# Unread opening products, early first operands and column-tiled filling products in a transformer-block forward and backward kernel

## The chip, the core and the metric

The kernel runs on one core of one Trainium2 chip. The metric is the device time of one execution in microseconds (us), as the median over several runs; lower is better.

Engine names in the profile: PE is the matrix engine (PEld its weight loads), DVE the vector engine, ACT the scalar engine, POOL is GpSimd, and SP the engine whose queue issues most transfers (SPq; in every view of it below they go out in the program's order). "Step", "round", "slot" and "row" are explained with the code.

## The reference

One transformer block with attention and a gated MLP in parallel, its output and all six gradients, in bf16: S = 2048 tokens, D = 448, 16 heads of 28, F = 1792.

```python
def _fwd_reference(A_x, A_wqkv, A_wo, B_x, B_w_gate, B_w_up, B_w_down):
    x = A_x
    xn = _layernorm(x, axis=-1)
    return x + _A_ref(xn, A_wqkv, A_wo) + _B_ref(xn, B_w_gate, B_w_up, B_w_down)
# _A_ref: qkv = xn @ wqkv; softmax(q k^T / sqrt(28)) v; @ wo
# _B_ref: (silu(xn @ w_gate) * (xn @ w_up)) @ w_down

def reference(A_x, A_wqkv, A_wo, B_w_gate, B_w_up, B_w_down, B_x, grad_out):
    _out, _vjp = jax.vjp(_f, A_x, A_wqkv, A_wo, B_w_gate, B_w_up, B_w_down)
    return (_out, *_vjp(grad_out))
```

## The kernel before

The kernel has three stages. An *opening* (to about 46 us) normalises x and projects the first Q, K and V. The *forward* (to about 606 us) runs 256 slots of scores, exponential and P times V, while "units" of other matrix work (MLP products, weight gradients) fill the gaps of PE. The *backward* runs 512 steps. A *row* of step k is the recomputed scores of step k and the products dO V^T of step k-1; ACT takes the exponential, DVE makes `ds`, PE makes dV and dK from both (`kv`). Four steps make a *round*, in which three of the four `ds` tiles are transposed by DMA and one on PE; the transposed tiles feed dQ (`dq`). The rest of PE's time goes to filling units again (`genb` tiles). Between forward and backward lies the *turn*.

The turn: six big loads (2.9 MB), then the first four rows, placed between the last five forward units; the row needs these loads.

```python
    def turn_loads():
        ...
        SP.dma_start(out=new_k(0, 0)[:], in_=KD_d[0, 0])
        for qc in range(4):
            SP.dma_start(out=new_q(0, qc)[:], in_=QD_d[0, qc])
        SP.dma_start(out=new_k(0, 1)[:], in_=KD_d[0, 1])
    ...
    for u in last[:-5]:
        run(u())
    k = n = 0
    for u in last[-5:]:
        for _ in u():
            n += 1
            if n in (8, 17, 25, 32):
                row(k); ew(k); k += 1
    K0 = k
    sp_flush()                     # two stores of the last transposed forward tile (odT)
    fwd.close()
    ...
    for x in pend:                 # DMA transposes of the first ds tiles, held back until here
        x()
    fT = bk.tile([P, 4, 2, 4, P], BF16, name="dsp", bufs=1)
    drip(("f",), [(fT[:, a:a + 2], fT_d[:, a:a + 2]) for a in (0, 2)], 10)
```

A transposed forward tile is stored by the same queue that later transposes `ds`, and the stores wait there for their own transpose to land (0.8 us in the profile of this kernel, 3.8 in that of the changed one), with everything issued after them behind:

```python
    def dst_dma(b, ds, qi):        # three of four ds tiles of a round
        SP.dma_start_transpose(out=dsT[b][:, qi]..., in_=ds[:]...)
    def ew(k):
        ...
        ds = dss[k - 1] = kq.tile([P, 2, 512], BF16, name="ds_sb", bufs=10)
        for j in range(2):
            DVE.tensor_tensor(out=ds[:, j], in0=dps.pop((k - 1, j))[:], in1=est[k - 1][:, j], op=ALU.mult)
        if qi < 2 or qi == 2 and b < NB // 4 - 1:
            pend.append(...) if bk is None else dst_dma(b, ds, qi)
```

A filling unit, one of five kinds (here the first kind in the backward, whose operand is `fT`):

```python
    def late_dw(c):
        have(("f",))
        ps = ps_g.tile([P, 2, P], FP32, name="genb")
        for t in range(NT):
            PE.matmul(ps[:dn], lhsT=xn_sp[:, t, d0:d0 + dn], rhs=fT[:, t // 4, :, t % 4, :], ...)
```

The softmax here doesn't subtract the row's maximum and nothing guards it: scores larger than these inputs give would overflow.

## Time and profile before

| | value |
|---|---|
| median of 3 runs | 1441.15 us (1439.99 to 1442.68) |
| span in the profile, granted clock | 1440.1 us, 0.985 |
| PE, ACT, DVE busy | 92%, 88%, 80% |
| exponential of the last forward slot / first ds / ds of step 511 | 606.52 / 617.22 / 1393.6 us |

Busy shares are averages over stages with different limits; the prediction below shows the stage lines and the turn of this profile. One more view of it matters, which I had not read closely before predicting: SP's own queue at the turn, in order of issue (start, how long the issues took, queue, line, operation, output<-input, count).

```profile
619.96 1.29 SPq L200 DMA_TRANSPOSE odT<-od  x1
...
622.78 0.32 SPq L206 DMA_DIRECT2D OT_d<-odT  x1
...
623.67 4.26 SPq L829 DMA_TRANSPOSE dsT<-ds_sb  x3
627.99 1.08 SPq L769 DMA_DIRECT2D dsp<-fT_d  x2
629.17 5.95 SPq L829 DMA_TRANSPOSE dsT<-ds_sb  x3
```

The reader is to see that the transpose of odT goes out at 619.96, when its operand is there, and the stores behind it wait 0.8 us more for odT to land.

### The profile page before, as it was taken

The page shows a single profiled execution, that of the slowest core. Times are in us where ns is not written, and L with a number is a line of the kernel's source. Part 1 is how long each engine was busy: PE and PEld are TensorE (multiplying, and loading weights), DVE is VectorE, ACT ScalarE, POOL GpSimd, SP SyncE. Part 2 cuts the span into 40 slices and gives each one's busy share as a digit, 9 for nine tenths or more (in the row PEclk, how much of TensorE's full clock was granted, in tenths as well). Part 3 has the DMA queues.
Part 4 walks back from the last instruction along what each step waited for, and adds up shares of the span by engine and source line. Part 5 has one row for each costly group of instructions (what it writes and reads, how often), then busy time and mean ns, then how long its engine had stood idle before and what let it go on. Part 6 is the DMA issues. An engine that isn't in the chain of part 4 may idle for free. (4 is left out here: it accounts for less than half of the span.)

```text
span 1440.1 us, 34682 instructions
## 1 busy us (share of the span) xinstructions
PE 1326.3 (92%) x12647; PEld 541.0 (38%) x12708; DVE 1151.8 (80%) x1997; ACT 1261.5 (88%) x2193; POOL 403.6 (28%) x561
## 2 busy tenths in 40 slices
PE   5889999999999999889999999999999999999996
PEld 2333333333333333333333434433443444444343
DVE  6667757666676676578998998888889999989988
ACT  5789988988889999869989989899989999989974
POOL 6464524464334454111112112201111011010006
PEclk9999999999999999989999999999999999999998
DMA  5796956796678586799999999999999999999971
GB/s 154 181 199 165 235 122 160 187 195 164 146 162 192 147 172 145 178 234 226 226 213 217 232 220 188 196 209 229 228 173 194 209 223 230 201 191 203 198 142 60
DMA packets 681179, 271.69 MB, mean 189 GB/s; under 512 B 606424, under 2 KB 655824, under 8 KB 681008
## 3 DMA queue, kind: packets, MB, share of 16 engines
q1 hardware_dynamic: 672576, 255.35, 87.1%
q0 software_dynamic: 7024, 13.82, 4.1%
q8 instruction: 100, 1.64, 0.5%
q14 instruction: 71, 0.58, 0.1%
q10 hardware_dynamic: 1408, 0.30, 0.1%
HBM read 65.09 MB, written 60.36 MB: 87 GB/s over the span
## 5 line engine op out<-in xcount | busy, mean ns | idle before, releaser
L842 DVE TENSOR_TENSOR ds_sb<-db,e_sb 128x512 bf16<-128x512 f32 x1024 | 646.8, 684 | 51.3 <-issue 21.1
L836 ACT ACTIVATE e_sb<-sb 128x512 bf16<-128x512 f32 x1024 | 554.8, 611 | 60.4 <-PE db L820 44.5
L612 ACT ACTIVATE eT<-s_w 128x1024 bf16<-128x1024 f32 x256 | 263.5, 1029 | 46.1 <-PE s_ps L609 43.1
L614 ACT ACTIVATE eT<-s_ps 128x512 bf16<-128x512 f32 x512 | 280.4, 612 | 0.0
L820 PE MATMUL db<-kd,qd 32*128 32x512 bf16 x1024 | 234.4, 384 | 8.2 <-DVE ds_sb L842 7.4
L812 PE MATMUL sb<-kd,qd 32*128 32x512 bf16 x1024 | 210.4, 387 | 5.1 <-DMA qd<-QD_d 3.3
L961 POOL TENSOR_TENSOR dq_acc<-dq_acc,dq_st 128x256 f32<-128x256 f32 x64 | 46.2, 721 | 455.4 <-ACT dq_st L959 455.4
L919 PE MATMUL acc<-ds_sb,qd 128*32 128x512 bf16 x1024 | 161.0, 391 | 0.0
L915 PE MATMUL acc<-e_sb,qd 128*32 128x512 bf16 x1024 | 158.8, 391 | 1.3 <-DVE dw_o L528 1.3
L902 ACT COPY dsT<-db 128x1024 bf16<-128x1024 bf16 x128 | 130.1, 1016 | 14.6 <-PE db L897 13.9
L380 POOL TENSOR_TENSOR nn<-nn,ag 128x512 f32<-128x512 f32 x56 | 71.2, 1271 | 252.2 <-DVE ag L378 243.7
L609 PE MATMUL s_ps<-QQ,KK 32*128 32x512 bf16 x512 | 125.4, 385 | 3.9
L1128 PE MATMUL genb<-wguT,dau_c 128*128 128x448 bf16 x448 | 117.5, 355 | 6.3 <-ACT dq_st L959 3.9
L609 PE MATMUL s_w<-QQ,KK 32*128 32x512 bf16 x512 | 100.3, 387 | 13.1 <-ACT eT L612 10.4
L812 PEld LDWEIGHTS <-qd 32*128 32x128 bf16 x1024 | 48.2, 91 | 149.4 <-issue 140.3
L421 PE MATMUL gen<-xn_t,f_sp 128*128 128x448 bf16 x416 | 91.8, 354 | 2.6 <-DVE nn L395 1.7
L421 PEld LDWEIGHTS <-f_sp 128*128 128x128 bf16 x640 | 55.7, 98 | 75.0 <-issue 31.9
L946 PE MATMUL genb<-dsT,kd 128*32 128x256 bf16 x2048 | 79.5, 275 | 1.9 <-DVE dqT L955 0.6
L897 PE MATMUL db<-ident_bf,ds_sb 128*128 128x128 bf16 x1032 | 79.4, 220 | 1.1 <-DVE ds_sb L842 1.1
L897 PEld LDWEIGHTS <-ds_sb 128*128 128x128 bf16 x1032 | 68.3, 99 | 24.1 <-issue 5.3
L451 PE MATMUL gen<-eT,VS 128*32 128x512 bf16 x1024 | 68.4, 384 | 5.5 <-DVE nn L395 3.3
L381 POOL TENSOR_TENSOR nn<-nn,tt 128x512 f32<-128x512 f32 x56 | 72.0, 1286 | 4.4
(167 smaller groups left out, 1911.0 us busy)
## 6 DMA issues: line engine op xcount, KB each, us to landing
F_d<-hda SPq DMA_DIRECT2D x56, 384.0 KB, 3.1
dau_c<-F_d SPq DMA_DIRECT2D x24, 512.0 KB, 4.4
qd<-QD_d SPq DMA_DIRECT2D x16, 512.0 KB
kd<-KD_d SPq DMA_DIRECT2D x16, 384.0 KB, 4.0
dsT<-ds_sb SPq DMA_TRANSPOSE x383, 4.3
dc<-dqkvT_d SPq DMA_DIRECT2D x12, 384.0 KB, 3.9
h_c<-F_d SPq DMA_DIRECT2D x8, 512.0 KB, 4.4
wT_d<-wT_f SPq DMA_DIRECT2D x14, 256.0 KB, 3.6
```

The source lines that it names most:

```text
L421: PE.matmul(ps[:, :D], lhsT=fsp[fc][:, t // 4, w, t % 4, :], rhs=rhs[:, t, :], start=(t == 0), stop=(t == NT - 1))
L609: PE.matmul(sp4[hh], lhsT=KK[g][r:r + HP, kt * P:(kt + 1) * P], rhs=QQ[g][r:r + HP, qsl], start=True, stop=True, tile_position=(r, 0))
L612: ACTE.activation(out=e2[0][:], in_=wide[:], func=ACT.Exp, scale=SCALE)
L614: ACTE.activation(out=e2[1][:, j], in_=sp4[2 + j], func=ACT.Exp, scale=SCALE)
L812: PE.matmul(s_ps[:], lhsT=qside[g, qc][r:r + HP, 0, qi * P:(qi + 1) * P], rhs=kside[g, kc][r:r + HP, 0, :], start=True, stop=True, tile_po ...
L820: PE.matmul(d_ps[:], lhsT=qside[g, qc][r:r + HP, 1, qi * P:(qi + 1) * P], rhs=kside[g, kc][r:r + HP, 1, :], start=True, stop=True, tile_po ...
L836: ACTE.activation(out=est[k][:, j], in_=sps.pop((k, j))[:], func=ACT.Exp, scale=SCALE)
L842: DVE.tensor_tensor(out=ds[:, j], in0=dps.pop((k - 1, j))[:], in1=est[k - 1][:, j], op=ALU.mult)
L897: PE.transpose(ps[:, c, :], ds[:, c // 4, (c % 4) * P:(c % 4 + 1) * P], ident_bf[:])
L902: ACTE.copy(out=o, in_=ps[:])
L915: PE.matmul(a[r:r + HP, :], lhsT=sp4[:, 1, r:r + HP], rhs=e[:, j, :], start=first, stop=last, tile_position=(0, r), skip_group_check=True)
L919: PE.matmul(a[r:r + HP, :], lhsT=sp4[:, 0, r:r + HP], rhs=ds[:, j, :], start=first, stop=last, tile_position=(0, r), skip_group_check=True)
```

## The change

Three parts. *Opening*: 24 products that nobody reads at the start, and 3 more before each of three projections, with the aim of a full clock of PE early on (granted 0.83 from 15 to 46 us in the profile before). *Turn*: 512 KB of operands for the first four rows are loaded at forward slot 240 into a tile of their own; row 0 goes ahead of the last six forward units; some DVE work of these units goes to ACT and POOL. *Tiles*: from step 160 on, a filling product that follows dV/dK is issued as four products on 32 columns each, so that the tile shape of PE needn't change between them (dV/dK to fill took 0.32 us, dV/dK to dV/dK of one shape 0.22).

```diff
+    def warm(ps, n):
+        for _ in range(n):
+            PE.matmul(ps[:], lhsT=ident_bf[:], rhs=ident_bf[:]...to_broadcast([P, 4, P]), start=True, stop=True)
...
+    warm(genx.tile([P, 512], FP32, name="gen"), 24)
...
-        proj(1, c + 1)
+        proj(1, c + 1, pre=3)
...
+        if i == NS - 16:
+            sp_flush()
+            first4 = wk.tile([P, S], BF16, name="qk_sp", bufs=1)[:]...
+            SP.dma_start(out=first4[:, 0:2], in_=KD_d[0, 0, :, 0:2])
+            SP.dma_start(out=first4[:, 2:4], in_=QD_d[0, 0, :, 0:2])
...
+            ks, qs = (first4[:, 0], first4[:, 2]) if k < 4 else (kside[g, kc][:, 0], qside[g, qc][:, 0])
...
-    for u in last[:-5]:
+    for u in last[:-6]:
         run(u())
-    k = n = 0
-    for u in last[-5:]:
+    n = 0
+    K0 = 5
+    row(0)
+    ew(0)
+    k = 1
+    for u in last[-6:]:
         for _ in u():
             n += 1
-            if n in (8, 17, 25, 32):
+            if n in (4, 20, 24, 32):
...
+    def mm(ps, lhsT, rhs, start, stop):
+        if not split:
+            PE.matmul(ps, lhsT=lhsT, rhs=rhs, start=start, stop=stop, skip_group_check=True)
+            return
+        for c in range(0, lhsT.shape[1], HP):
+            PE.matmul(ps[c:c + HP], lhsT=lhsT[:, c:c + HP], rhs=rhs, start=start, stop=stop,
+                      tile_position=(0, c), skip_group_check=True)
...
+        split = m > 1 and k >= 160
```

(The five unit kinds call `mm`; the last od unit's copy and product go to ACT and POOL, its small operations to POOL, the last dW_o copy to ACT.)

More of the change, by code (lines that the diff above doesn't have):

```diff
@@ L267, in qkv_open, with qkv_unit @@
         VS[g] = wk.tile([P, NT, P], BF16, name="VS")
-    def qkv_unit(g, tq, sc, act=False):
+    def warm(ps, n):
+        for _ in range(n):
+            PE.matmul(ps[:], lhsT=ident_bf[:], rhs=ident_bf[:].unsqueeze(1).to_broadcast([P, 4, P]), start=True, stop=True)
+    def qkv_unit(g, tq, sc, act=False, pre=0):
         if g not in QQ:
@@ L274, in qkv_unit @@
         ps = new_gen([P, 512], FP32, name="gen")
+        warm(ps, pre)
         for c in range(4):
@@ L503, in mid3 @@
         dl = wk.tile([P, 3, 16], FP32, name="dl")
-        DVE.tensor_copy(out=dOl, in_=prod[:])
-        DVE.tensor_tensor(out=prod[:], in0=prod[:], in1=t[:, 0].rearrange("p q (h r) -> p (q h) r", r=HP), op=ALU.mult)
+        end = (g, qc) == (G - 1, 3)
+        (ACTE.copy if end else DVE.tensor_copy)(out=dOl, in_=prod[:])
+        (POOL if end else DVE).tensor_tensor(out=prod[:], in0=prod[:], in1=t[:, 0].rearrange("p q (h r) -> p (q h) r", r=HP), op=ALU.mult)
         yield 0
@@ L508, in mid3 @@
         yield 0
-        DVE.tensor_scalar(out=dl[:, 1, :], in0=dl[:, 0, :], scalar1=-1.0, scalar2=None, op0=ALU.mult)
-        DVE.tensor_copy(out=dOl[:, :, 28], in_=dl[:, 1, :])
-        DVE.tensor_tensor(out=dl[:, 2, :], in0=dl[:, 1, :], in1=dOl[:, :, 28], op=ALU.subtract)
-        DVE.tensor_copy(out=dOl[:, :, 29], in_=dl[:, 2, :])
+        eng = POOL if (g, qc) == (G - 1, 3) else DVE
+        eng.tensor_scalar(out=dl[:, 1, :], in0=dl[:, 0, :], scalar1=-1.0, scalar2=None, op0=ALU.mult)
+        eng.tensor_copy(out=dOl[:, :, 28], in_=dl[:, 1, :])
+        eng.tensor_tensor(out=dl[:, 2, :], in0=dl[:, 1, :], in1=dOl[:, :, 28], op=ALU.subtract)
+        eng.tensor_copy(out=dOl[:, :, 29], in_=dl[:, 2, :])
         tT = wk.tile([P, 2, 4, P], BF16, name="odT")
@@ L527, in dwo_unit @@
         o = wk.tile([P, D], BF16, name="dw_o", bufs=1)
-        DVE.tensor_copy(out=o[:], in_=ps[:, :D])
+        (ACTE.copy if g == G - 1 else DVE.tensor_copy)(out=o[:], in_=ps[:, :D])
         for hh in range(4):
@@ L632, in T, with proj @@
             run(T_unit(xnT, xn_t, t))
-    def proj(tq, sc, act=False):
-        run(qkv_unit(0, tq, sc, act))
+    def proj(tq, sc, act=False, pre=0):
+        run(qkv_unit(0, tq, sc, act, pre))
     def stats4(cc):
@@ L728 @@
         slot(i)
+        if i == NS - 16:
+            sp_flush()
+            first4 = wk.tile([P, S], BF16, name="qk_sp", bufs=1)[:].rearrange("p (a s) -> p a s", a=4)
+            SP.dma_start(out=first4[:, 0:2], in_=KD_d[0, 0, :, 0:2])
+            SP.dma_start(out=first4[:, 2:4], in_=QD_d[0, 0, :, 0:2])
         if kq is None and i > NS - 8 and not fill.stream and fill.cur is None:
@@ L811, in row @@
                 r = HP * (2 * hp + j)
-                PE.matmul(s_ps[:], lhsT=qside[g, qc][r:r + HP, 0, qi * P:(qi + 1) * P],
-                          rhs=kside[g, kc][r:r + HP, 0, :], start=True, stop=True, tile_position=(r, 0))
+                PE.matmul(s_ps[:], lhsT=qs[r:r + HP, qi * P:(qi + 1) * P],
+                          rhs=ks[r:r + HP], start=True, stop=True, tile_position=(r, 0))
                 sps[k, j] = s_ps
@@ L816, in row @@
             g, hp, kc, qc, qi = steps[k - 1]
+            ks, qs = (first4[:, 1], first4[:, 3]) if k <= 4 else (kside[g, kc][:, 1], qside[g, qc][:, 1])
             for j in range(2):
@@ L819, in row @@
                 r = HP * pv(2 * hp + j)
-                PE.matmul(d_ps[:], lhsT=qside[g, qc][r:r + HP, 1, qi * P:(qi + 1) * P],
-                          rhs=kside[g, kc][r:r + HP, 1, :], start=True, stop=True, tile_position=(r, 0))
+                PE.matmul(d_ps[:], lhsT=qs[r:r + HP, qi * P:(qi + 1) * P],
+                          rhs=ks[r:r + HP], start=True, stop=True, tile_position=(r, 0))
                 dps[k - 1, j] = d_ps
@@ L864 @@
                 k += 1
-    K0 = k
     sp_flush()
@@ L880, in late_dw @@
         for t in range(NT):
-            PE.matmul(ps[:dn], lhsT=xn_sp[:, t, d0:d0 + dn], rhs=fT[:, t // 4, :, t % 4, :],
-                      start=(t == 0), stop=(t == NT - 1))
+            mm(ps[:dn], xn_sp[:, t, d0:d0 + dn], fT[:, t // 4, :, t % 4, :], t == 0, t == NT - 1)
             if t < NT - 1:
@@ L890 @@
     dq_acc = bk.tile([P, S // 2], FP32, name="dq_acc", bufs=1)
+    split = False
+    def mm(ps, lhsT, rhs, start, stop):
[5 more added lines that the diff above has]
+                      tile_position=(0, c), skip_group_check=True)
     def tr_unit(b):
@@ L1010, in dwq_unit @@
         for t in range(NT):
-            PE.matmul(ps[:dn, :], lhsT=xn_sp[:, t, d0:d0 + dn], rhs=dsp[g][:, t].rearrange("p k r -> p (k r)"),
-                      start=(t == 0), stop=(t == NT - 1))
+            mm(ps[:dn, :], xn_sp[:, t, d0:d0 + dn], dsp[g][:, t].rearrange("p k r -> p (k r)"), t == 0, t == NT - 1)
             if t < NT - 1:
@@ L1066, in y_unit @@
         tsl = slice(ti * P, (ti + 1) * P)
-        mm = [(ych[ch, half][:, i, tsl], wd_sb[:, half * NH + i, :]) for i in range(NH)]
+        ops = [(ych[ch, half][:, i, tsl], wd_sb[:, half * NH + i, :]) for i in range(NH)]
         if half:
-            mm += [(ych[ch, 3][:, i, tsl], wo_sb[:, i, :]) for i in range(G)]
+            ops += [(ych[ch, 3][:, i, tsl], wo_sb[:, i, :]) for i in range(G)]
         ps = ps_g.tile([P, 512], FP32, name="genb")
-        for i, (l, r) in enumerate(mm):
-            PE.matmul(ps[:, :D], lhsT=l, rhs=r, start=(i == 0), stop=(i == len(mm) - 1))
-            if i < len(mm) - 1:
+        for i, (l, r) in enumerate(ops):
+            mm(ps[:, :D], l, r, i == 0, i == len(ops) - 1)
+            if i < len(ops) - 1:
                 yield 189
@@ L1127, in dx_unit @@
         for i in range(n):
-            PE.matmul(ps[:, :D], lhsT=d[:, i // 2, i % 2, tsl], rhs=dxs["w", fq][:, i // 2, i % 2, :],
-                      start=(i == 0), stop=(i == n - 1))
+            mm(ps[:, :D], d[:, i // 2, i % 2, tsl], dxs["w", fq][:, i // 2, i % 2, :], i == 0, i == n - 1)
             if i < n - 1:
@@ L1171, in dc_unit @@
         for i in range(3 * G - 3):
-            PE.matmul(ps[:, :D], lhsT=dcs[t // 4][:, i, (t % 4) * P:(t % 4 + 1) * P], rhs=dxs["wq"][:, i, :],
-                      start=(i == 0), stop=(i == 3 * G - 4))
+            mm(ps[:, :D], dcs[t // 4][:, i, (t % 4) * P:(t % 4 + 1) * P], dxs["wq"][:, i, :], i == 0, i == 3 * G - 4)
             if i < 3 * G - 4:
@@ L1270 @@
             fill_step(R3)
+    split = False
     while stream:
```

## The prediction

> **What bounds the kernel now.** I read the page first, then the busy time by stage, then the timeline at the opening, at the turn from forward to backward, and in single rounds of the backward. The page says that no engine is alone at its limit, and where the slow clock lies.
>
> ```profile
> PE 1326.3 (92%) x12647; PEld 541.0 (38%) x12708; DVE 1151.8 (80%) x1997; ACT 1261.5 (88%) x2193; POOL 403.6 (28%) x561
> PEclk9999999999999999989999999999999999999998
> ```
>
> The reader is to see that the clock is nearly full everywhere: whatever warm-up gives is confined to a few short dips. By stage (columns: busy time and instructions of PE, weight loads, DVE, ACT, POOL; granted clock, DMA share, GB/s):
>
> ```profile
> 15.00:46.00 31.00, 24.28 (x161) 8.48 (x163) 19.47 (x44) 23.29 (x36) 15.34 (x13) 0.83 0.28 58
> 46.00:606.00 560.00, 520.86 (x3766) 201.41 (x3822) 374.34 (x644) 504.45 (x785) 248.19 (x332) 1.00 0.76 175
> 606.00:640.00 34.00, 26.37 (x220) 9.58 (x220) 23.24 (x42) 20.12 (x37) 3.23 (x6) 0.85 0.84 211
> 880.00:1395.00 515.00, 494.76 (x5680) 208.44 (x5678) 470.60 (x798) 472.25 (x881) 65.18 (x97) 0.99 1.08 202
> ```
>
> The forward (46 to 606) has PE and ACT at 93% and 90%. The turn (606 to 640) is the hole: ACT idles 13.9 of 34 us, DVE 10.8. In the backward PE is at 96%, DVE and ACT at 91 to 92%: three engines in lockstep, so time taken from one of them mostly becomes waiting there. The turn's timeline shows the wait that the change aims at (start, length, engine, line, operation, output<-input; brackets: idle before it, releaser):
>
> ```profile
> 610.02 1.91 SPq L724 DMA_DIRECT2D qd<-QD_d  x4
> ...
> 614.10 0.39 PE L812 MATMUL sb<-kd,qd 32*128 32x512 bf16 x2 [3.27 <-DMA qd<-QD_d]
> ...
> 614.52 1.09 ACT L836 ACTIVATE e_sb<-sb 128x512 bf16<-128x512 f32 x2 [6.00 <-PE sb L812]
> ...
> 617.22 1.28 DVE L842 TENSOR_TENSOR ds_sb<-db,e_sb 128x512 bf16<-128x512 f32 x2
> ...
> 622.98 0.39 PE L915 MATMUL acc<-e_sb,qd 128*32 128x512 bf16 x2 [1.28 <-DVE dw_o L528]
> ```
>
> The first backward scores wait for a load issued 4 us earlier, and the first dV/dK product waits for a DVE copy queued behind other DVE work. One backward round (four steps, 5.63 us):
>
> ```profile
> 1147.94 2.48 DVE L842 TENSOR_TENSOR ds_sb<-db,e_sb 128x512 bf16<-128x512 f32 x4 [0.16 <-issue]
> 1147.95 0.38 PE L915 MATMUL acc<-e_sb,qd 128*32 128x512 bf16 x2
> ...
> 1148.27 0.36 PE L1128 MATMUL genb<-wguT,dau_c 128*128 128x448 bf16 x1
> 1148.57 0.39 PE L812 MATMUL sb<-kd,qd 32*128 32x512 bf16 x2
> 1148.57 0.49 PE L820 MATMUL db<-kd,qd 32*128 32x512 bf16 x2
> 1148.99 0.93 PE L1128 MATMUL genb<-wguT,dau_c 128*128 128x448 bf16 x4
> ```
>
> From a dV/dK pack to the filling product is 0.32 us; from one dV/dK pack to the next (128x32 tiles both) 0.22; also from dV/dK to dQ, which has 128x32 tiles too, 0.22. So changing the tile shape costs about 0.10 us. The 0.49 and the 0.42 us up to the next fills show that the following row lost 0.10 us on its second db tile.
>
> [...] the dQ packs here (four 32-column tiles, 256 wide) follow each other at 0.109 us[...], so loads of narrow tiles stay hidden. [...] granted 0.50 in stretches of 3.4 or 6.8 us (20.6 to 27.4, 41.1 to 44.5, 614.5 to 617.9, 624.8 to 628.2, 631.6 to 635.0).
>
> **The change, part by part.**
>
> *Opening products.* 24 unread 512-column products run from about 1.4 us, and 3 more before each of three projections. The first transposes start at 9.35 us. At half speed a product of 512 columns takes 0.427 us (the first eight projection products took 2.83 us in all, at spacings of 0.42), at full speed 0.216. [...] The 8 projection products then save 8 x 0.21 = 1.7 us, but DVE has statistics before the Q copy, so the first scores (15.46) come about 1.1 us sooner. That is then lost: the transposes at 18.58 and 20.42 wait for GpSimd's normalisation, whose chain begins with a queue of weight loads and does not depend on PE. What can last is the clock from 20.6 to 27.4 and 41.1 to 44.5, where PE is busy 5.9 and 2.9 us and ACT waits for it (2.5 and 2.4 us before the exponentials at 24.15 and 43.85). Removing both dips would give 3 us at most; but the dip at 20.6 follows a sparse stretch that lies before the first three extra products, and if the clock is down they cost 3 x 0.21 = 0.6 us more. I book 1.5 us.
>
> *Early first operands.* Two loads of 256 KB at the last 16th forward slot serve the first four rows; row 0 moves ahead of the transposes at 609.73. It can go at about 609.0 (the last forward products end at 608.9) instead of 614.10: 5.1 us. DVE's first ds then follows the od product: start 611.4 instead of 617.2. Also taken from DVE in this chain: 0.43 + 0.69 (copy and product), 0.17 + 0.20 + 0.18 + 0.20 (small ones), 0.61 (dw_o) = 2.5 us, to ACT and POOL. In DVE's new order, od, 2 ds, prod 0.69, 2 ds, reduce 0.61, 2 ds, with ds at 0.62: the sixth ds ends at 611.4 + 3.7 + 1.3 = 616.4, against 622.4 before: 6.0 us. Row 4 still needs the big loads (its query tile is the second, the first was there at 614.1; I estimate 615), but they are no longer first. The 16 dW_o products end about 617.4, ACT copies, and the first dV/dK starts near 618.2 instead of 622.98: 4.8 us. One row more is done by then (five, not four), and the dips at 624.8 and 631.6, which follow idle PE, may go or shrink (up to 1.7 us each). I book 6.5 us.
>
> *Column tiles.* Built, the PE order shows 424 filling products (240, 80 and 20 of 448 columns, 84 of 384) cut in tiles, 1,230 extra products and as many extra loads. They belong to some 80 units, each with one dV/dK-to-fill change removed: 80 x 0.10 = 8 us of PE time. A pack may take up to 0.01 us longer than one wide product (dV/dK packs come at 0.216 or 0.226), and the exit to the next row 0.01. What reaches the end depends on the kind of round, which I sorted by length. Rounds of 5.63 us (19): DVE idles only 0.16, at a point upstream of the fill, and the next row waits 0.10 for DVE: gain 0. Rounds of 5.91 (11, ACT copies the unit): the same 0.10 us wait swallows it: 0, or -0.02. Rounds of 5.69 (9): 0.07 is swallowed, some 0.05 gained as they approach 5.63: 0.5. Ends of a K chunk (13, 6.3 to 6.7 us): the change of shape lies in the last step of the round and ACT then waits 0.52 for the next row: 0.07 each, 0.9. Weight-gradient rounds (12, 6.4 us, PE waits 0.1): 0.05 each, 0.6. Rounds with transposes: 0. Sum 1.5 to 2, booked as 1.5.
>
> Sum: 1.5 + 6.5 + 1.5 = 9.5 us; 1441.2 - 9.5 = 1431.7.
>
> **The rivals.** (a) *Column tiles pay in full.* PE waits for others only about 34 of 760 us in the backward (640 to 1400, the view of waits), which speaks for PE as the bound; then 8 instead of 1.5 us: 1425. Against it stands DVE's idle of 0.16 us in the commonest round. (b) *Column tiles cost.* [...] The dQ packs speak against it. (c) *The turn's gain is taken back.* Row 4 and the dW_o products sit behind the db buffers, which DVE frees, and behind the 2.9 MB of big loads; if the first dV/dK only comes at 620, 3 us remain: 1435. For it: the DMA is at 382 GB/s just then. (d) *The opening is hidden wholly* behind GpSimd and DMA, or the extra products run at half clock: 1433.
>
> **Range and chances.** The turn is the surest part (4 to 8.5), the opening -0.5 to 3.5, the tiles -1 to 6. Together a central 9 to 10 and 8 times in 10 between 4 and 15: 1426 to 1437. Two per cent is 28.8 us; all three parts at their upper ends give 18. So faster by over 2%: 0.02; within: 0.97; slower: 0.01.
>
> **What would show it.** In the changed profile: the first backward scores near 609 without a DMA wait, the first ds near 611.5, the first dV/dK near 618 (each shifted by what the opening gave); dV/dK to fill 0.22 us, and the next row's wait grown from 0.10 to about 0.20 in the 5.63 us rounds, which keep their length; 6.4 us rounds shortened by 0.05; clock below 0.95 between 20 and 27 gone or not, decides the opening. I am wrong if the rounds of 5.63 us shorten by 0.1, if tile packs follow at much over 0.19 us, or if the first dV/dK comes no earlier than 621.

The 1.7 us of the eight projection products supposed that the 24 bring the clock up before them; when that would be was not shown. (In the changed profile the 24 start 0.43 us apart up to 4.25 us and 0.216 after it, the first record of a granted clock, 1.00, is at 4.19 us, and from 11.0 to 14.4 us it is 0.50.) Two statements stand on measured numbers. That loads of narrow tiles stay hidden: the 0.109 us between dQ packs of 256 columns is half of the 0.216 of a 512-column product. That dips follow idle PE: in the 3.4 us before the five dips PE was busy 73%, 59%, 13%, 49% and 76%.

## The result, and the profile after

The changed kernel took 1442.3 us (median of 4 runs, 1441.2 to 1442.9); the kernel before took 1440.6 beside it (4 runs, 1439.4 to 1442.7). The ratio is 1.001, 95% interval 0.9992 to 1.0027: the same. I had predicted 1431.7 with a range of 1426 to 1437, so the 9.5 us that I had summed up are not there.

The page of the changed kernel, busy time and granted clock in 40 slices:

```profile
PE 1339.5 (93%) x13971; PEld 556.0 (39%) x13971; DVE 1148.8 (80%) x1990; ACT 1260.8 (88%) x2195; POOL 406.6 (28%) x566
PEclk9999999999999999989999999999999999999998
```

The clock row reads as before. By stage (columns as in the prediction):

```profile
15.00:46.00 31.00, 25.78 (x205) 10.03 (x205) 21.55 (x48) 25.18 (x39) 15.56 (x13) 1.00 0.31 66
46.00:606.00 560.00, 526.16 (x3800) 200.65 (x3801) 371.96 (x642) 502.87 (x782) 248.90 (x332) 1.00 0.75 175
606.00:640.00 34.00, 24.82 (x202) 9.88 (x198) 19.09 (x32) 19.49 (x35) 4.74 (x10) 0.85 0.88 211
880.00:1395.00 515.00, 494.00 (x6870) 218.44 (x6859) 469.88 (x796) 470.50 (x881) 65.30 (x97) 0.99 1.11 202
```

In the opening the granted clock is 1.00 from 15 to 46 us in this trace, 0.83 in the kernel before (ten later traces with these products do not repeat that, see below). But the turn, where the change aimed at the holes, is emptier than before: PE 24.82 us instead of 26.37, DVE 19.09 instead of 23.24 (some 2.5 us of DVE's work went to ACT and POOL by the change itself), at the same mean clock of 0.85. Its timeline says where:

```profile
608.48 0.39 PE L826 MATMUL sb<-qk_sp 32*128 32x512 bf16 x2
...
610.92 1.28 DVE L857 TENSOR_TENSOR ds_sb<-db,e_sb 128x512 bf16<-128x512 f32 x2
...
617.99 0.39 PE L826 MATMUL sb<-kd,qd 32*128 32x512 bf16 x2 [2.55 <-DMA qd<-QD_d]
...
621.50 0.61 PE L942 MATMUL acc<-e_sb,qd 128*32 128x512 bf16 x2 [0.62 <-ACT dw_o L535]
...
632.48 0.58 PE L913 MATMUL genb<-dsp,xn_t 128*128 128x256 bf16 x2 [2.98 <-DMA dsp<-fT_d]
```

The first scores come at 608.48 without a wait and the first `ds` at 610.92, as predicted. Then row 4 waits for the big loads until 617.99, the first dV/dK starts at 621.50, only 1.5 us earlier than before, and a wait that the kernel before did not have stands at 632.48: the first filling product waits 2.98 us for its own operand `fT`. SP's queue in the changed kernel, to lay beside the one above:

```profile
616.66 1.38 SPq L200 DMA_TRANSPOSE odT<-od  x1
...
622.50 0.32 SPq L206 DMA_DIRECT2D OT_d<-odT  x1
...
623.41 4.11 SPq L844 DMA_TRANSPOSE dsT<-ds_sb  x3
627.58 1.06 SPq L782 DMA_DIRECT2D dsp<-fT_d  x2
628.74 7.57 SPq L844 DMA_TRANSPOSE dsT<-ds_sb  x3
```

The transpose of odT is issued 3.3 us earlier, but it lands no earlier (its stores go at 622.50 instead of 622.78). The big loads are in flight then; that they hold it up was not tested. So the first transpose of `ds` is issued at 623.41 instead of 623.67, and `fT` is loaded at 627.58 instead of 627.99. PE, ACT and DVE are 6 us ahead, and the queue isn't: the backlog between a first `ds` and its transpose grew from 6.45 to 12.49 us.

In the common backward round after step 160 the tiles do what was worked out:

```profile
1144.60 0.38 PE L942 MATMUL acc<-e_sb,qd 128*32 128x512 bf16 x2
...
1144.82 0.36 PE L916 MATMUL genb<-wguT,dau_c 128*32 128x448 bf16 x4
...
1145.16 0.55 PE L835 MATMUL db<-kd,qd 32*128 32x512 bf16 x2
...
1145.64 0.94 PE L916 MATMUL genb<-wguT,dau_c 128*32 128x448 bf16 x16
```

dV/dK to the fill is 0.22 us instead of 0.32, sixteen 32-column products of 448 take 0.94 us as four whole ones did (0.93), so no cost of their loads shows, and the next row's second tile takes 0.55 instead of 0.49: the time won becomes waiting for DVE, and the round is 5.64 us long.

### The profile page after: what moved, and what is told of

Its sections match the earlier page's. It is cut to its first block, busy times and chain, and to the rows that moved or that the text cites. A ratio compares the mean times of both kernels' runs of the same rounds, so it can differ in the third digit from the quotient of the medians. Undisturbed runs are those within 1.5% of the kernel's fastest.

```text
span 1440.4 us, 37274 instructions
## 1 busy us (share of the span) xinstructions
PE 1339.5 (93%) x13971; PEld 556.0 (39%) x13971; DVE 1148.8 (80%) x1990; ACT 1260.8 (88%) x2195; POOL 406.6 (28%) x566
## 5 line engine op out<-in xcount | busy, mean ns | idle before, releaser
L616 PE MATMUL s_w<-QQ,KK 32*128 32x512 bf16 x512 | 99.7, 385 | 12.3 <-ACT eT L619 10.4
L616 PEld LDWEIGHTS <-KK 32*128 32x128 bf16 x1024 | 29.2, 91 | 114.4 <-issue 111.7
```

The lines of the kernel that those rows point to most:

```text
L616: PE.matmul(sp4[hh], lhsT=KK[g][r:r + HP, kt * P:(kt + 1) * P], rhs=QQ[g][r:r + HP, qsl], start=True, stop=True, tile_position=(r, 0))
```

## The experiments

**How to read them.** Single runs of one kernel scattered far more here than in the first result: the kernel before, run 44 times on three chips, took 1437.5 to 1448.0 us, and each kernel's own six runs spread by 2 to 5 us (standard deviation). A median alone can't settle 2 us. So I cut every profiled run at the same marks: the exponential of forward slot 32 and of slot 255 (the last), and the `ds` of backward steps 0, 12, 36, 152 and 511. The columns from "ds 0" to "ds 152" count from the exponential of slot 255; "queue" is the issue of the first transpose of `ds`; "half" is the time between slot 255 and step 152 in which the records give a granted clock of 0.50.

| kernel | slot 32 | slot 255 | ds 0 | queue | ds 12 | ds 36 | ds 152 | half | 152 to 511 | ratio (95%) |
|---|---|---|---|---|---|---|---|---|---|---|
| before | 99.7 | 606.5 | 10.7 | 17.2 | 31.2 | 65.5 | 244.4 | 13.7 | 542.7 | 1 |
| changed | 94.6 | 606.1 | 4.8 | 17.3 | 33.3 | 67.4 | 244.1 | 17.1 | 542.1 | 1.001 (0.9992-1.0027) |
| e1 turn only | 99.9 | 607.9 | 4.8 | 15.7 | 30.7 | 67.0 | 245.6 | 23.9 | 540.9 | 1.0017 (0.9994-1.0040) |
| e2 opening only | 98.9 | 607.9 | 11.5 | 18.0 | 32.7 | 68.5 | 243.3 | 27.3 | 543.4 | 1.0036 (1.0017-1.0054) |
| e3 tiles only | 100.1 | 611.6 | 11.1 | 17.5 | 32.0 | 67.4 | 244.2 | 17.1 | 540.2 | 1.0008 (0.9985-1.0031) |
| e4 fill from 13 | 100.2 | 611.2 | 4.8 | 16.9 | 24.8 | 66.4 | 245.9 | 20.5 | 540.0 | 1.0020 (1.0001-1.0040) |
| e5 fT first | 96.8 | 611.0 | 4.8 | 18.7 | 27.6 | 70.4 | 248.8 | 30.7 | 538.7 | 1.0029 (1.0007-1.0051) |
| e6 fT first, row 4 late | 98.2 | 607.8 | 4.8 | 18.0 | 27.7 | 68.5 | 248.6 | 23.9 | 541.3 | 1.0017 (0.9991-1.0044) |
| e7 = e6, no opening | 100.9 | 608.2 | 4.8 | 17.1 | 26.7 | 68.0 | 243.7 | 23.9 | 538.5 | 0.9969 (0.9946-0.9992) |
| e8 24 products only | 99.3 | 609.4 | 12.1 | 18.5 | 33.3 | 67.4 | 245.4 | 13.7 | 540.9 | 1.0000 (0.9976-1.0023) |
| e9 changed, PE transposes | 98.5 | 608.1 | 4.8 | 17.2 | 29.0 | 63.9 | 244.8 | 23.9 | 540.3 | 0.9984 (0.9955-1.0012) |
| e10 before, PE transposes | 98.9 | 609.0 | 11.1 | 17.5 | 32.5 | 68.5 | 244.5 | 20.5 | 547.7 | 1.0013 (0.9990-1.0037) |
| e11 changed, stores moved | 99.8 | 609.4 | 4.8 | 13.7 | 29.0 | 63.3 | 242.8 | 17.1 | 538.5 | 1.0009 (0.9985-1.0034) |
| e12 all relief, no opening | 100.5 | 611.0 | 4.8 | 13.5 | 25.1 | 63.2 | 241.2 | 10.2 | 543.9 | 0.9970 (0.9945-0.9996) |
| e13 before, fewer loads | 98.6 | 607.7 | 10.9 | 17.4 | 31.8 | 66.1 | 239.1 | 17.1 | 543.4 | 0.9978 (0.9956-1.0000) |
| e14 changed, fewer loads | 97.4 | 607.8 | 4.8 | 16.8 | 31.1 | 68.3 | 243.5 | 34.1 | 540.6 | 0.9972 (0.9951-0.9993) |
| e15 changed again | 97.5 | 608.1 | 4.8 | 16.8 | 32.5 | 67.0 | 243.6 | 30.7 | 542.7 | 1.0011 (0.9979-1.0043) |
| e16 candidate | 96.2 | 603.0 | 4.8 | 13.5 | 24.0 | 65.7 | 242.0 | 20.5 | 546.1 | 0.9960 (0.9940-0.9981) |
| e17 changed, no opening | 101.1 | 609.7 | 4.8 | 15.9 | 30.6 | 67.2 | 244.3 | 23.9 | 539.7 | 0.9987 (0.9960-1.0014) |
| e18 e16 + opening | 97.6 | 612.9 | 4.8 | 13.5 | 25.9 | 66.6 | 247.1 | 23.9 | 539.0 | 0.9997 (0.9967-1.0027) |

**Part of the scatter is half-clock stretches.** Over the 152 runs of the experiments, each group's mean taken out, time and mean granted clock correlate at -0.59, so about a third of the variance goes with the clock. The stretches are 3.41 us long or a multiple of it (but for the last, which the span's end cuts), on a grid whose phase differs from run to run (edges at 13.79, 20.62 and 27.44 us in the profile before, at 4.19, 11.02 and 14.43 in the changed one). I laid that grid through all 20 traces and took PE's busy share in each full-speed window: after a window of 0.9 or more the clock was halved 0 times out of 6191, after 0.8 to 0.9 27 times out of 975, after 0.6 to 0.7 58 of 186, after less than 0.5 49 of 58. One such window cost 1.4 to 1.5 us where it falls on the tail (in the changed profile PE is busy all through it): the tail behind step 511 takes 46.5 to 46.7 us in the kernels without a window there and 47.9 to 48.1 in those with one. So a stall of 2 to 3 us costs itself, and may cost up to 1.5 us more right after it (an estimate from these counts and the tail).

### The three parts alone, and a later first fill (one set)

**e1_turn_only.** The changed kernel without its opening products and with the products whole:

```diff
-    warm(genx.tile([P, 512], FP32, name="gen"), 24)
...
-        proj(1, c + 1, pre=3)
+        proj(1, c + 1)
...
-        split = m > 1 and k >= 160
+        split = False
```

> Only the turn part is applied (early first operands, rows moved ahead, DVE work moved to ACT and POOL); no opening products, no column tiles. Theory T1 (the turn's gain is handed back at the first filling product, which now waits about 3 us for its own operand, the load of fT): the first ds comes about 6 us earlier than in the kernel before, round 8 about 3 us earlier, and by step 16 nothing of it is left; total within 1.5 us of the kernel before, ratio 0.999 to 1.001. Rival R1 (the prediction's: the turn pays its 6.5 us and another part costs them): 1434, ratio 0.9955. Rival R2 (what is left of it is lost to half-clock stretches that fall by chance): between -3 and +1, and step 16 about 3 us early.

Measured: 1443.4 us (before 1440.0 in this set), ratio 1.0017. The first `ds` is 5.9 us nearer to the last forward exponential, by step 12 the lead is 0.6 us, by step 36 it is gone. The first fill waited 3.37 us for `fT`. T1 holds; R1 (1434) is out. R2 is out as the main cause, since the lead is lost at that wait, though it has half-clock windows behind it.

**e2_open_only.** The kernel before plus `warm`, the 24 products and `pre=3`, as in the diff above.

> Only the 24 opening products and the three times 3 before projections are added to the kernel before. Theory T2 (the forward is held by something that does not depend on its start, so it swallows the early lead): about 5 us ahead at forward slot 64, less than 1 us ahead at the last forward slot; total within 1 us, ratio 0.9993 to 1.0007. Prediction's step: 1.5 us gained, ratio 0.999. Rival R3 (the products cost): +1 us or more, with a half-clock stretch in the Q and K projections that delays slot 0.

Measured: 1445.0 us, ratio 1.0036: slower than any of the expectations but R3's. The profiled run shows a lead of 0.8 us at slot 32, 0.9 at slot 64 (T2 wanted 5 there) and none by slot 255. More on this below.

**e3_tiles_only.** The kernel before plus `mm` and `split`, as in the diff above.

> Only the column tiles from step 160 on are applied. Theory T3: they pay 2 to 3.5 us as the round-by-round working said (0.05 to 0.11 in the longer rounds, none in the common one): total 1438 to 1439.5, ratio 0.9975 to 0.9985. Rival (b) of the prediction, tiles cost: +1 us or more. Rival (a), they pay in full: -8 us, ratio 0.9945.

Measured: 1441.1 us (1437.4 to 1445.7), ratio 1.0008 with an interval of 0.9985 to 1.0031: inconclusive in total time. By the marks the stretch in which tiles exist, step 152 to 511, is 2.4 us shorter than in the kernel before (540.2 instead of 542.7). Over all 20 traces, with the median of each round of four steps: tiles take 2.07 us off the 87 rounds from step 160 on. The rounds that end a K chunk and the weight-gradient rounds lose 0.10 to 0.11 each, the 5.69 us rounds lose 0.05, and the common 5.63 us rounds grow by 0.01. By the rounds T3 is right and rivals (a) and (b) are out; total time doesn't confirm it.

**e4_fill_from_13.** The changed kernel, whose first filling unit may begin one round later:

```diff
-            if 9 <= k < NB and cur is None:
+            if 13 <= k < NB and cur is None:
...
-            if 9 <= k < NB:
+            if 13 <= k < NB:
```

> The changed kernel whole, but filling units may begin from step 13 and not from step 9, so the first of them starts one round later and finds its operand loaded. T1: the wait of about 3 us for the load of fT disappears, step 12 begins 3 us earlier than in the changed kernel, no other round is longer because two rounds near step 20 have no filling work anyway: total 1438 to 1440, 3 to 4 us under the changed kernel. Rival R4 (the stall only moves, to the transposed ds or to the clock): within 1 us of the changed kernel.

Measured: 1443.2 us, ratio 1.0020. The wait for `fT` is gone and the `ds` of step 12 is at 24.8 instead of 33.3 us: the turn's 6 us are all there, and more. By step 36 they are lost: steps 12 to 36 take 41.6 us instead of 34.1, with 10.8 us of half clock in them and a new wait of a dQ product for a transposed `ds`:

```profile
652.11 0.62 PE L973 MATMUL genb<-dsT,kd 128*32 128x256 bf16 x16 [1.69 <-DMA dsT<-ds_sb]
```

R4 holds: the stall moved on to the next thing that the same queue delivers.

### Relieving the turn (second set)

**e5_ft_first.** The changed kernel with the loads of `fT` ahead of the pending transposes:

```diff
-    for x in pend:
-        x()
     fT = bk.tile([P, 4, 2, 4, P], BF16, name="dsp", bufs=1)
...
-    drip(("f",), [(fT[:, a:a + 2], fT_d[:, a:a + 2]) for a in (0, 2)], 10)
+    for a in (0, 2):
+        SP.dma_start(out=fT[:, a:a + 2], in_=fT_d[:, a:a + 2])
+    for x in pend:
+        x()
```

> The changed kernel, with the two loads of fT (operand of the first filling product) issued ahead of the three pending transposes of ds instead of behind them, about 4 us earlier on the queue. From the last forward exponential to the ds of step 12 the kernel before took 31.3 us, the changed one 33.3, the one whose filling began a round later 24.8. T1 (the fT wait is the step that took the turn's gain): that stretch falls to 27 to 29 us, dV/dK to the first fill is 0.25 us instead of 3.0, and steps 12 to 36 stay at 34 to 35 us when no half-clock window falls in them. R4 (the stall moves on, because the DMA queue is what is full): the stretch shortens, but steps 12 to 36 take over 36 us with a wait for transposed ds. In total time T1 gives 1438 to 1440, R4 1442; single runs of one kernel scatter by 2 to 4 us, so the verdict is read from the stretches.

Measured: 1448.2 us, ratio 1.0029. Step 12 is reached at 27.6 us and the fill doesn't wait, as T1 said; steps 12 to 36 then take 42.8 us, as R4 said, instead of 34.1. In that stretch PE waits 1.7 us and DVE 3.1 us for transposed `ds`, and 16.6 us of half clock fall there; at 1.4 to 1.5 us a window the clock alone would be some 7 us of the 8.7 lost (an estimate).

**e6_ft_first_row4_late.** As e5, and row 4 goes to the main loop:

```diff
-    K0 = 5
+    K0 = 4
...
-            if n in (4, 20, 24, 32):
+            if n in (4, 20, 24):
```

> As the kernel before this one in the list, and row 4 is also taken out from between the dW_o products and left to the main loop, so that dW_o, its copy and the first dV/dK no longer stand behind the big load. T1b: first dV/dK about 3 us earlier relative to the first ds (7 to 8 us after it instead of 10.6), the stretch from the last forward exponential to step 12 falls to 25 to 27 us. Rival R5 (ACT and DVE, not PE, then set the end, because row 4's exponentials wait for the same load anyway): stretch within 1 us of e5_ft_first.

Measured: 1445.4 us, ratio 1.0017. Steps 0 to 4 take 8.6 us instead of 11.7 (changed) and 12.1 (e5). Over all nine traces of the changed turn with row 4 in its place they take 8.9 to 12.1, so row 4 costs 0.3 to 3.5 us there: T1b's 3 us are the upper end. Step 12 comes at 27.7 us all the same, within 1 us of e5, as R5 said.

**e7_same_no_opening.** As e6, without the opening products (the first two hunks of e1).

> As e6_ft_first_row4_late, without the 24 opening products and the three times 3 before projections. If the opening products cost what their single run suggested (1445.0 against 1440.0, ratio 1.0036), this is 3 to 5 us faster than e6_ft_first_row4_late: 1434 to 1437. Rival R6 (that ratio came from half-clock windows that fell by chance elsewhere): within 1.5 us of e6_ft_first_row4_late.

Measured: 1438.8 us, ratio 0.9969 (0.9946 to 0.9992), the first kernel that is faster than the kernel before, and 7.3 us in the mean under e6, from which only the opening products are gone.

**e8_open_24_only.** As e2 with `proj(1, c + 1)` left as it was.

> The kernel before with the 24 opening products alone, without the three times 3 before projections. If the 9 later products cost (0.22 to 0.43 us each on the path to the opening's exponentials, 2 to 4 us), this is 2 us or more under e2_open_only's 1445; if the 24 cost, it is at 1444 to 1446; under R6 (chance) within 1.5 us of the kernel before.

Measured: 1442.4 us, ratio 1.0000 (0.9976 to 1.0023). This hints that the nine later products, and not the 24, cost e2 its time, but the two intervals overlap, so that stays a hint.

### The queue (third set)

By now the time from the first transpose of `ds` on the queue to that of step 152 was 231.8 to 235.5 us in all ten kernels, while the time from the first `ds` to the `ds` of step 152 lay between 231.8 and 244.0.

**e9_after_pe_transposes.** In the first three rounds the third `ds` tile too is transposed on PE:

```diff
-        for qi in (3,) if b < NB // 4 - 1 else (2, 3):
+        for qi in (3,) if 3 <= b < NB // 4 - 1 else (2, 3):
...
-            if qi < 2 or qi == 2 and b < NB // 4 - 1:
+            if qi < 2 or qi == 2 and 3 <= b < NB // 4 - 1:
...
-        ds = dss[k] if qi == 3 or k == NB - 2 else dss.pop(k)
+        ds = dss[k] if qi == 3 or qi == 2 and k < 12 or k == NB - 2 else dss.pop(k)
```

> The changed kernel; in the first three rounds of the backward the third ds tile too is transposed on TensorE, as the fourth is, so the queue has 3 of the first 9 transposes fewer. Theory TQ: the in-order queue that transposes ds by DMA paces steps 0 to 152. In all ten kernels so far the time from its first to its 115th transpose is 231.8 to 235.5 us, with the queue 94% busy, while the first ds moved by 6 us and its first transpose by nothing (623.4 to 623.7). With 3 transposes fewer the queue is up to 6 us ahead: the wait of a ds for its transpose at step 12 is under 5 us, first ds to the ds of step 152 falls from 239.3 to 233 to 236, total 1437 to 1440. Rival R7 (TensorE, DVE and ACT pace these steps; the backlog on the queue is only slack in the buffers): the added transposes and copies cost, first ds to step 152 stays at 239 to 244.

Measured: 1440.7 us (before 1444.0 in this set), ratio 0.9984. Step 36 comes at 63.9 us, 3.4 earlier than in the changed kernel, and its queue goes from its first transpose to that of step 36 in 52.0 us instead of 56.8: 4.8 us for three transposes fewer. But the lead is there by step 12 (29.0 against 33.3): `fT` stands behind two transposes instead of three, and the first fill waits 0.38 us for it instead of 2.98. Steps 12 to 36 take 34.9 us without a wait for a transposed `ds`, so this run doesn't show that the queue paces them. By step 152 nothing is left (244.8), and first `ds` to step 152 is 240.0 us where TQ wanted 233 to 236. TQ falls as the cause for the whole stretch.

**e10_before_pe_transposes.** The same edit on the kernel before.

> Control: the same edit on the kernel before. Under TQ it helps there as well, since the queue paces it too (first ds to step 152: 233.7 us): 229 to 233. Under R7 it costs 1 to 3 us in the first three rounds and gives nothing later.

Measured: 1445.5 us, ratio 1.0013; first `ds` to step 152 is 233.4 us, not 229 to 233. It cost 2.9 us by step 36, of which two half-clock windows are a part. That cost isn't clear either: the other unchanged turns reach step 36 at 65.5 to 68.5 (e2). So three early transposes fewer give nothing here, as R7 said. That the compute engines pace these steps doesn't follow; e13 below speaks against it.

**e11_after_stores_moved.** The two stores that wait for odT go to GpSimd's queue:

```diff
-    sp_flush()
+    for o, i in late:
+        POOL.dma_start(out=o, in_=i)
+    late.clear()
     fwd.close()
```

> The changed kernel; the two stores of the last transposed forward tile (they wait about 4 us for that transpose to land) go to GpSimd's queue, so they no longer stand ahead of the first transposes of ds. TQ: the first transpose of ds is issued near 619 to 620 instead of 623.4, the load of fT follows about 4 us sooner as well, and both the wait before the first fill and the backlog fall: first ds to step 152 falls from 239.3 to about 235, total 1438 to 1440. R7: the first fill waits less, but step 152 stays where it was (239 after the first ds).

Its queue:

```profile
619.95 1.31 SPq L200 DMA_TRANSPOSE odT<-od  x1
621.31 0.58 SPq L524 DMA_DIRECT2D QD_d<-od  x1
623.08 4.35 SPq L844 DMA_TRANSPOSE dsT<-ds_sb  x3
```

Measured: 1443.6 us, ratio 1.0009. From odT's transpose to the first of `ds` is 3.1 us now, where the changed kernel had 6.75. Counted from slot 255 the queue starts at 13.7 instead of 17.3, the fill waits 0.19 us for `fT`, and step 36 comes at 63.3 us, 4.1 earlier, all of it won by step 12 (29.0 against 33.3). At step 152 it is still 1.3 us ahead. The place that TQ named is right, its reach is not.

**e12_all.** e7 with both edits (stores moved, three transposes on PE).

> Both edits, with fT loaded first, row 4 left to the main loop and no opening products: tiles and the turn's idea with its queue relieved. TQ: first ds to step 152 in 229 to 233 us, first ds as early as in the changed kernel; total 1431 to 1435, ratio 0.992 to 0.996 of the kernel before. R7: as the kernel with the row left to the main loop and no opening products, ratio 0.997.

Measured: 1438.5 us, ratio 0.9970. Step 152 comes at 241.2 us, 3.2 before the kernel before, the best of the correct kernels. First `ds` to step 152 took 236.4 us, not the 229 to 233 of TQ. A wait that the backlog still causes, at step 143:

```profile
835.90 1.29 DVE L856 TENSOR_TENSOR ds_sb<-db,e_sb 128x512 bf16<-128x512 f32 x2 [1.50 <-DMA dsT<-ds_sb]
```

DVE can't write a new `ds`, because the next of the ten buffers hasn't been transposed yet.

### What paces steps 36 to 152, and repeats (fourth set)

**e13_before_fewer_loads.** Wrong on purpose: the filling units of steps 36 to 170 read one chunk of operands four times (the reference check fails on the first output alone, with a relative error of 1.22), so some 8 MB of loads vanish and every compute instruction stays:

```diff
     def load_y(ch, half):
+        if ch:
+            ych[ch, half], ych[ch, 2 + half] = ych[0, half], ych[0, 2 + half]
+            return
```

> Wrong on purpose in one output: the kernel before, where the filling work of steps 36 to 170 reads its first chunk of operands four times instead of loading four chunks, so some 8 MB of loads are gone between step 20 and step 152; every instruction of the compute engines stays. Fourteen kernels took 241.2 to 248.8 us from the last forward exponential to the ds of step 152 (unchanged turn 243.3 to 245.4, changed turn 241.2 to 248.8), though the changed turn makes the first ds 6 us earlier. Theory TD (transfers, the loads and the DMA transposes together, pace this stretch): with the loads gone the unchanged turn falls from 244.4 to 238 to 242. Rival R8 (the compute engines pace it, half-clock windows included): 243 to 246 as ever.

DMA share and GB/s are the last two figures of each line, first of the kernel before, then of e13, in the same stretch:

```profile
640.00:860.00 220.00, 205.53 (x2357) 86.30 (x2356) 200.40 (x326) 200.08 (x372) 35.02 (x56) 0.99 1.16 223
```

```profile
640.00:860.00 220.00, 207.17 (x2440) 88.31 (x2433) 205.74 (x336) 205.67 (x384) 35.97 (x58) 1.00 1.08 193
```

Measured: 1440.6 us (before 1444.2), ratio 0.9978. Step 152 comes at 239.1 us, 5.3 earlier than in the kernel before, with half-clock time no shorter. The backlog of the queue, 7.3 us at step 152 in the kernel before, is 1.35 us, which is also its least value late in the backward: no backlog. TD holds for the unchanged turn.

**e14_after_fewer_loads.** The same edit on the changed kernel.

> The same on the changed kernel, wrong on purpose in the same output. TD: the turn's gain now lasts, so this is 3 to 6 us shorter than e13_before_fewer_loads from the last forward exponential to step 152 (it was 244.1 against 244.4 with the loads), less whatever the early wait for fT (3 us) takes. R8: within 1 us of e13_before_fewer_loads.

Measured: 1440.3 us, ratio 0.9972; step 152 at 243.5 us, 4.4 later than e13 where TD wanted it 3 to 6 earlier. So TD failed here. The first fill waits for `fT` again (1.42 us here), and the lead over e13 is down to 0.7 us by step 12. Behind it the clock is halved for 34.1 us against 17.1 in e13; five windows more, at 1.4 to 1.5 us each, are some 7 us (an estimate), enough for the 5.1 us lost from step 12 on. From step 36 on the rounds of both kernels have the lengths of undisturbed ones, those with a half-clock window apart.

**e15_after_again.** The changed kernel, unedited.

> The changed kernel unedited, because four runs on another chip were all there was. If the sum of what the stages keep (opening 0, turn 0, tiles 2.4 to 2.7 us) is right: 2 to 3 us under the kernel before, ratio 0.998 to 0.9985. If the opening products cost, as 1445.0 and 1445.4 in two experiments suggested: 1 to 3 us over it.

Measured: 1444.5 us (1437.6 to 1452.6) against 1444.2, ratio 1.0011, as the first time. The sum of what the stages keep (0.998) is not confirmed.

**e16_tiles_and_turn_queue.** e7 with the stores moved (e11's edit).

> A candidate to beat both: column tiles, turn with fT first, row 4 left to the main loop and the last stores off the queue, no opening products, no transposes moved to TensorE. Two kernels close to it were at ratio 0.997. Expected 0.994 to 0.998; if it is over 0.999, what seemed to help there was chance.

Measured: 1437.9 us against 1444.2, ratio 0.9960 (0.9940 to 0.9981). It beats both kernels, by some 6 us. Its queue starts as early as in e11, but step 36 comes only at 65.7 us: steps 12 to 36 take 41.7 us, with 10.3 us of half clock, and DVE waits 4.1 us and PE 2.2 us for transposed `ds`.

### The opening products once more (fifth set)

**e17_after_no_opening** and **e18_candidate_with_opening.** e17 is the changed kernel less the opening products (first two hunks of e1); e18 is e16 with them.

> The changed kernel without its opening products; turn and tiles as they are. Theory TO (the opening products cost in total time, as e2 against the kernel before, +5.3 us of mean, and e6 against e7, +7.3, say): 3 to 7 us under the changed kernel, ratio to the kernel before 0.996 to 0.999 where the changed kernel had 1.0011. Rival R9 (the stages say so: a lead of 1.7 us at forward slot 32, gone by slot 255, so the two pairs are chance): ratio 1.000 to 1.002.

> e16_tiles_and_turn_queue (ratio 0.996) with the opening products put back. TO: ratio 0.999 to 1.001, 4 to 7 us slower. R9: 0.995 to 0.997.

Measured: e17 1441.6 us, ratio 0.9987 (0.9960 to 1.0014); e18 1443.2 us, ratio 0.9997 (0.9967 to 1.0027); before 1442.5 in this set. So four pairs differ by the opening products alone, and in all four they cost: 5.3 us (e2), 7.3 (e6 over e7), 3.5 (1.0011 less 0.9987 of 1442) and 5.3 (0.9997 less 0.9960). Two are clear of the scatter by themselves (e2's interval lies above 1; 7.3 has a standard error of 1.7), the other two are not; all four have one sign, and their mean is 5.3. TO holds for the 24 and the nine together; for the 24 alone (e8) no cost shows (ratio 1.0000).

The traces show part of it. With the products (11 traces) slot 32 comes at 98.1 us in the mean, without them (9 traces) at 99.5: the 1.5 us that I had booked, with a standard error of 0.7. The dip at 20 to 28 us, which was to go, stays in 10 of the 11 (8 of the 9 without have it). The one at 40 to 48 stays in 5 of the 11 (7 of the 9), and the lead hangs on it: slot 32 comes at 99.3 in those five and at 97.0 in the other six. At slot 255 it is 609.1 with and 608.3 without, a difference that is not clear of the scatter (standard error 1.0). The largest loss lies at slots 124 to 128, 13.2 us with and 11.4 without. A weight-gradient product there waits for a transposed tile, first the kernel before, then e2:

```profile
310.81 0.36 PE L421 MATMUL gen<-dy_t,f_sp 128*128 128x448 bf16 x1 [1.87 <-DMA f_sp<-hda]
```

```profile
311.37 0.36 PE L426 MATMUL gen<-dy_t,f_sp 128*128 128x448 bf16 x1 [2.63 <-DMA f_sp<-hda]
```

A half-clock window follows there in 9 of the 11 traces with the products and in 2 of the 9 without. Slots 192 to 200 lose 1.0 us more and 240 to 248 win 0.6 back. The traces hold a likely reason that I had overlooked. `prof e2_open_only --dma` lists a queue that the profile calls "instruction", whose packets have 16 KB (queue q8: 100 packets, 1.64 MB). One such packet falls 1.4 to 2.1 us after the exponential of slot 124 in all 11 traces with the products, while that transpose is awaited, and none there in the 9 without, where it comes at slot 126. The same happens at the end of the forward: a packet 0.4 to 0.8 us after the exponential of slot 255 in all 11 and in none of the 9, and the turn's query loads, which stand behind a store that waits for a transpose, are issued 3.9 to 4.7 us after that exponential with the products and 3.5 without. So the unread products seem to shift where these packets fall. That the packets delay the transposes isn't tested, and e8, which shows no cost, has them at the same places.

By the end of the forward the traces account for a net loss of 0.8 us (1.5 won, then 2.2 lost, rounded), total time says 5.3. The granted clock of every run accounts for more: in all four pairs it is lower with the products, by 0.0027, 0.0030, 0.0017 and 0.0033 (e8 against the kernel before: 0.0001 higher). The mean of 0.0027 over 1441 us is 7.7 us of half clock, 2.3 windows, and at 1.4 to 1.5 us each some 3.3 us (an estimate; only e2's difference is clear of the scatter by itself). Why more windows are halved with the products stays open.

## Why the prediction was wrong

*The opening.* I booked 1.5 us, and by slot 32 it is 1.5 us, but not by the way that I had worked out: the first of the two dips that were to go stays in 10 of 11 traces, the second in 5. So the agreement is partly luck. I had also misread the eight projection products: their starts are 0.43 us apart only up to 13.5 us and 0.216 after it, so full speed could save 0.9 us there, not 1.7. The step that failed for the total is "What can last is the clock". I had looked for what could swallow the lead in the first 46 us and took the 560 us of the forward for a stage that hands on what it is given. It does not: its waits for transposed tiles are of their own, the lead is gone by slot 255, and in total time the products cost 5 us, with a lower granted clock over the whole run. The sign of this term was wrong. Rival (d), hidden wholly, was nearer and still too kind.

*The turn.* First scores 608.48 (predicted 609.0), first `ds` 610.92 (611.4), end of the sixth `ds` 616.53 (616.4): this step was right. The step that failed first is "Row 4 still needs the big loads [...] I estimate 615". They came at 617.99. (Without the opening products, in e1 and e17, row 4 comes 10.3 and 10.5 us after slot 255 instead of 11.9, so part of this is the opening's doing.) So dW_o, which stood behind that row, was done 3 us later than predicted, and the first dV/dK came at 621.50 instead of 618.2, past the 621 that I had named as proof against me. The larger fault is that I stopped reading at the first dV/dK. Behind it stand two things that one queue delivers, `fT` and the transposed `ds`, and this queue got no head start (623.41 against 623.67). The four traces of the unrelieved changed turn (changed, e1, e15, e17) reach step 152 at 244.4 us in the mean, the five of the unchanged turn with all loads (before, e2, e3, e8, e10) at 244.4: of the 6 us nothing is left. Where a reader could have seen it: SP's queue in the profile before has hardly a gap from 623.67 on, with 6 us of backlog. Its issues are long: at least 1.23 us for the transpose of a 256 KB tile of `ds`, where the load of a 512 KB tile took 0.57 (median), and with the loads in between 2.0 to 2.2 us per transpose (54.8 to 58.6 us for the first 27).

The mechanism, as far as shown: up to step 12 it is the wait for `fT` (e4 takes it away, and the lead is whole at step 12); e9 and e11, too, win their 4.3 us there. Where step 12 is reached early (e4 to e7, e12, e16, e18, at 24.0 to 27.7 us), steps 12 to 36 take 38.2 to 42.8 us instead of 34.1, with waits for transposed `ds` in each (on PE up to 2.2 us, on DVE up to 4.1) and 3.4 to 16.6 us of half clock. So up to step 36 it is the queue and the half-clock windows behind its stalls; how the loss divides between them isn't settled. From 36 to 152 transfers pace the unchanged kernel (e13: step 152 comes 5.3 us earlier without some 8 MB of loads); for the changed one the half-clock stretches that follow its stalls have at least as large a share (e14), and how the two divide there stays open. Rival (c) named the right kind of loss and put it at half its size.

*The tiles.* Right in mechanism. Booked 1.5 us, measured 2.07 from round medians: ends of a K chunk give 0.10 each instead of 0.07, weight-gradient rounds 0.11 instead of 0.05. The common round gives nothing, as worked out.

*The sum.* For 9.5 us of gain the runs show 2 from the tiles, about 0 from the turn and a loss of some 5 from the opening products. That is a loss of 3, where the changed kernel measured +0.1% of 1442, 1.4 us, with an interval of -1.2 to +3.9.

*The range.* I took the time as exact to a few tenths. Its standard deviation from run to run was 3 us in the later sets, and about a third of the variance goes with the granted clock (correlation -0.59).

## What to carry to other kernels

When a change lets the engines start earlier, look up whether the transfer queue that feeds the next steps starts earlier too; if its first issue doesn't move, the gain can become mere backlog, as here (6.45 us to 12.49), and the wait show up one or two stages on. Read such a queue by itself, for gaps: one without a gap, with a standing distance between producing a tile and transposing it, may be a bound even though no engine names it, and taking transfers away (as in e13) tests that. Where single runs scatter by more than the effect, a median can't tell, so measure stages between fixed marks in several traces.
